# Sparse attention and a rational-activation MLP on one core: the order of the strided casts, and the first and the last group of the MLP in pieces

## The chip, the cores and the metric

The kernel runs on one core of a Trainium2 chip. The metric is the device time of one execution in microseconds (us). A core has five engines that run side by side, each with its own in-order stream of instructions: TensorE (PE, with its weight loads shown apart as PEld), VectorE (DVE), ScalarE (ACT), GpSimd (POOL) and SyncE (SP). Transfers are issued by GpSimd and by SyncE, each with a queue of its own, and are carried out by 16 DMA engines that both queues share.

## The reference

q, k and v have 8 batches, 8 heads, 576 positions and 64 columns. Heads 0 to 3 see a local window, heads 4 to 7 a strided pattern. The result, 4608 tokens of 512 columns, goes through an MLP with 2048 hidden columns and a rational activation.

```python
mask_local = (rel >= 0) & (rel < 32)
mask_strided = (rel >= 0) & (pos[None, :] % 32 == pos[:, None] % 32)
scores = np.where(masks[None, :, :, :], scores, -1000000000.0)
attn = softmax(scores); x = attn @ v          # then heads side by side: 4608 x 512
h = x @ w_in
P = a[0] + a[1] * h + a[2] * h2 + a[3] * h3
Q = 1.0 + np.abs(b[0]) * np.abs(h) + np.abs(b[1]) * h2
g = P / (Q + 1e-06)
return g @ w_out
```

## The kernel before

The kernel is written as a list of operations, each with an engine, an assumed duration, a sort key and the tiles that it reads and writes. `schedule` is a planner: it plays the list on a model of the engines and the DMA queues, always takes the ready operation with the smallest key, and so fixes the order of each engine's stream. `emit` then writes those streams with the semaphore waits that the tiles ask for. The order is therefore fixed before the run; an engine whose next operation isn't ready waits, even if a later one is. A change of one assumed time or one dependence can move operations anywhere in the streams. Where the planner sees TensorE without work at the start or at the end, it puts in filler matmuls on a constant tile (`filler`, L136).

Per batch the work is this:

- `casts(b)` issues on GpSimd the transfers that bring q, k and v in as bf16. For the first two batches q and k of the local heads, then of the strided heads, go straight into SBUF tiles h (L562); for later batches they are copied as bf16 into DRAM (L515). V of the local heads is five transfers (L546 and four times L550), V of the strided heads two (L569). In the kernel before, the five for local V stand between the local pair and the strided pair of q and k.
- `loads(b)` brings q and k into the layout that the scores need (tq, tk). For the first two batches `loads_pe` does it with TensorE transposes (L612, L649), copied out of PSUM by ScalarE for q (L631, L661) and by VectorE for k (L633, L663). For later batches SyncE issues DMA transposes of q and k (L678) and, for the local heads, two small copies each (L689).
- `attention(b)` has four units: local, strided, strided, local. Each computes scores on TensorE (L775 and L784, or L860 and L868), a row maximum on VectorE (L794, L875), subtracts it by a matmul (L801, L882), takes the exponential on ScalarE (L807, L888), transposes it (on TensorE for two batches: L819, L900; then by DMA on SyncE: L825, L908), multiplies with V (L837, L931 with the sums L918), and divides on VectorE (L846 and L848, L938 and L941).
- `turn` transposes the result (L731 local, L738 strided); ScalarE copies it into XT (L754), the tokens side by side in a ring of three chunks of 512.

The MLP takes the tokens in nine chunks of 512 and the hidden columns in four groups of eight blocks. `mlp1(c)` computes a block of h with four matmuls (L966), and ScalarE takes it out of PSUM (L972). When the eight blocks of a group are there, VectorE works on 128 x 4096 elements at once: the absolute value (L992), two operations for the denominator (L994, L996), then ScalarE takes its logarithm and the exponential of the negative (L1020, L1022) while VectorE makes the numerator by Horner's rule (L1023, L1025, L1026, L1027, L1028); L1029 multiplies the two. The last group of the last chunk goes another way: ScalarE takes the absolute value and the first step (L988, L989), the logarithm and exponential are in two halves (L1001, L1003), VectorE does L1004, L1005 and L1006 over the whole, then adds the last coefficient in halves (L1013) and multiplies with the reciprocal in pieces of half, quarter and quarter (L1015). `mlp2(c)` multiplies with w_out (L1055), takes the result out of PSUM (L1067, and L1065 for two pieces of the last chunk) and stores it (L1074). In the last chunk the matmuls are ordered by piece of g, so that they follow the pieces as they become ready.

Of the kernel before, what the change touches and what calls it, by code (L numbers as in the profile page):

```python
# [6 lines left out]
Alu = mybir.AluOpType  # L7
# [362 lines left out]
def bass_strided_sparse_attn__then__act_rational_pade_kernel(nc, q, k, v, moe_w_in, moe_w_out, moe_a, moe_b, out):  # L370
# [163 lines left out]
    def casts(b, after=None):  # L534
        after = after if after else [()] * 7
        key = b * 576 - 1500 if b > 1 else -1e5 + 3e4 * b
        for n in range(2):
            T_q[b][n].new()
            T_k[b][n].new()
        for n in range(2):  # L540
            if n:
                vl = vL_of[b] = R_vL.next()
                vt = vLs_of[b] = vts.setdefault(vl.name, Tile(f"vs{vl.name}")).new()
                va = vl.prev + list(after[2])
                VB = v.offset + b * H * S * D
                P.op("pool", lambda e: e.dma_start(  # L546
                    vl.t[:, 0, :, 0:64], bass.AP(tensor=v.tensor, offset=VB, ap=[[D, KW], [S * D, HL], [1, D]])),
                    0.8, key, w=[vt], dma=0.6, after=va)
                for h in range(HL):
                    P.op("pool", lambda e, h=h: e.dma_start(  # L550
                        vl.t[:, 1:NQ, h, 0:64],
                        bass.AP(tensor=v.tensor, offset=VB + (h * S + STRIDE) * D,
                                ap=[[D, KW], [64 * D, NQ - 1], [1, D]])),
                        0.8, key, w=[vt], dma=0.95, after=va)
            if b < NPE:
                h = stage[b, n] = R_h.next()
                hv = h.t[:, :, :].rearrange("p g c -> p (g c)")
            for i, (s_t, d_t, t) in enumerate(((q, q16, T_q[b][n]), (k, k16, T_k[b][n]))):
                if b >= NPE:
                    bulk(s_t, d_t, b, HL * n, HL, H, t, key, after[3 * n + i])  # L560
                    continue
                P.op("pool", lambda e, s_t=s_t, hv=hv, i=i, n=n: e.dma_start(  # L562
                    hv[0:TP, i * HL * TW:(i + 1) * HL * TW].rearrange("p (h c) -> p h c", c=TW),
                    bass.AP(tensor=s_t.tensor, offset=s_t.offset + (b * H + HL * n) * S * D,
                            ap=[[TW, TP], [S * D, HL], [1, TW]])),
                    0.8, key, w=[t], dma=1.75, after=list(after[3 * n + i]) + h.prev)
        vS = vS_of[b] = R_vS.next()
# [384 lines left out]
    def mlp1(c):  # L952
# [3 lines left out]
        groups = []  # L956
        for g in range(NG):
            h = R_h.next()
            for f in range(g * G, g * G + G):
                ph = PTile("ph", 1)  # L960
                key = base + f * 16
# [8 lines left out]
                if f == 7:  # L970
                    early = o
                P.op("act", lambda e, f=f, ph=ph, h=h: e.activation(  # L972
                    h.t[:, f % G, :], ph.f, AF.Copy),
                     0.6, key, r=[ph], w=[h])
# [7 lines left out]

            def dv(fn, dur, **kw):
                P.op("dve", fn, dur, key, **kw)
            if end:
                y = R_h.next()
                yy = y.t[:, :, :]
                P.op("act", lambda e, zz=zz, hh=hh: e.activation(zz, hh, AF.Abs), 3.6, key, r=[h], w=[z])  # L988
                P.op("act", lambda e, yy=yy, hh=hh: e.activation(yy, hh, AF.Identity, bias=a_ap[2], scale=a_ap[3]),  # L989
                     3.7, key, r=[h, T_co], w=[y])  # L990
            else:
                dv(lambda e, hh=h.t, zz=z.t: e.tensor_scalar(zz.bitcast(u16)[:, :, :], hh.bitcast(u16)[:, :, :], 0x7FFF, None,  # L992
                                                             op0=Alu.bitwise_and), ts + 0.15, r=[h], w=[z])
            dv(lambda e, zz=zz, uu=uu: e.tensor_scalar(uu, zz, b1_ap, b0_ap, op0=Alu.mult, op1=Alu.add),  # L994
               ts + 0.28, r=[z, T_b], w=[u])
            dv(lambda e, zz=zz, uu=uu: e.tensor_tensor(uu, uu, zz, op=Alu.mult), tt, r=[z], m=[u])  # L996
            if end:
                yh = [Tile(f"yh{i}") for i in range(2)]
                for i in range(2):
                    ui = u.t[:, 4 * i:4 * i + 4, :]  # L1000
                    P.op("act", lambda e, ui=ui: e.activation(ui, ui, AF.Ln, bias=eps1, scale=1.0),  # L1001
                         1.9, key, r=[T_co, u], w=[yh[i]])
                    P.op("act", lambda e, ui=ui: e.activation(ui, ui, AF.Exp, scale=-1.0), 1.85, key, m=[yh[i]])  # L1003
                dv(lambda e: e.tensor_tensor(yy, yy, hh, op=Alu.mult), tt, r=[h], m=[y])  # L1004
                dv(lambda e: e.tensor_scalar(yy, yy, a_ap[1], None, op0=Alu.add), ts + 0.22, m=[y])  # L1005
                dv(lambda e: e.tensor_tensor(yy, yy, hh, op=Alu.mult), tt, r=[h], m=[y])  # L1006
                yt = [Tile(f"yt{i}") for i in range(2)]
                for p0, p1 in ((0, 4), (4, 6), (6, 8)):
                    i = p0 // 4
                    tp = Tile(f"hp{p0}")  # L1010
                    if p0 % 4 == 0:
                        yi = y.t[:, p0:p0 + 4, :]
                        dv(lambda e, yi=yi: e.tensor_scalar(yi, yi, a_ap[0], None, op0=Alu.add),  # L1013
                           ts / 2 + 0.22, r=[y], w=[yt[i]])
                    dv(lambda e, p0=p0, p1=p1: e.tensor_tensor(  # L1015
                        h.t[:, p0:p1, :], y.t[:, p0:p1, :], u.t[:, p0:p1, :], op=Alu.mult),
                       tt * (p1 - p0) / G, r=[yt[i], yh[i], h], w=[tp])
                    groups.append((h, p0, p1, tp))
                continue
            P.op("act", lambda e, uu=uu: e.activation(uu, uu, AF.Ln, bias=eps1, scale=1.0),  # L1020
                 0.833 * W / 1000 + 0.28, key, r=[T_co], m=[u])
            P.op("act", lambda e, uu=uu: e.activation(uu, uu, AF.Exp, scale=-1.0), 0.833 * W / 1000 + 0.19, key, m=[u])  # L1022
            dv(lambda e, zz=zz, hh=hh: e.tensor_scalar(zz, hh, a_ap[3], a_ap[2], op0=Alu.mult, op1=Alu.add),  # L1023
               ts + 0.28, r=[h, T_co], m=[z])
# [119 lines left out]
```

## Time and profile before

| | |
|---|---|
| time, median of 3 runs | 405.66 us (403.07 to 407.18) |
| the profiled execution | 407.25 us, span from the first to the last instruction 405.4 us |
| mean granted clock of TensorE | 0.977 |
| VectorE busy | 359.2 us, 89% of the span |
| ScalarE busy | 291.0 us, 72% |
| chain that ended last | VectorE 69%, TensorE 20%, issue 5%, DMA 3% |
| read from and written to HBM | 39.29 MB and 16.52 MB, 138 GB/s over the span |

The profile is of one execution. Busy times are sums over an engine's instructions. The chain that ended last is followed back from the last instruction, at each step to what released it; "issue" in it is time in which an engine waited for nothing that the profile shows. A row of a group gives the line, the engine, the operation and the shapes, the number of instructions, their busy time in us, the mean of one in ns, and the idle time of the engine just before them with what ended most of it. A row of the timeline gives the start and the length in us. A row of a transfer gives its size and the time from issue to landing. Line numbers are those of the kernel before.

### The profile page before, as it was taken

Reading aid. Unit: us, or ns where it says so; the run is one execution under the profiler, and the core shown is the slowest. Engines: PE = TensorE matmul, PEld = TensorE weight load, DVE = VectorE, ACT = ScalarE, POOL = GpSimd, SP = SyncE. Lnnn points to the kernel's source line nnn. Section 1 sums busy time; section 2 is a strip of 40 time slices with the busy share of each in tenths; the row PEclk is TensorE's granted clock in tenths of the full one; section 3 lists DMA queues with packets and bytes.
Section 4 is the critical chain, followed back from the end, with each engine's and each line's share of the span. In section 5 each row is a group of like instructions: output and inputs, shape, how many; then the busy total and the mean of one; then the engine's idle time right before and its main releaser. Section 6 shows DMA issues by size and latency. Waiting matters only on the chain.

```text
span 405.4 us, 8744 instructions
## 1 busy us (share of the span) xinstructions
PE 370.7 (91%) x3874; PEld 184.9 (46%) x3874; DVE 359.2 (89%) x315; ACT 291.0 (72%) x316; POOL 93.6 (23%) x136
## 2 busy tenths in 40 slices
PE   6989774899999999989999999999999999999596
PEld 2463542544554455445444544544454444344242
DVE  4571996799999799999999999999999999999981
ACT  2355593597929695868786878686969888898961
POOL 8991000700171037007213420001000200100100
PEclk9899997899998999999999999999999999999999
DMA  8999999986499939999995997013500200200202
GB/s 100 186 199 176 223 150 98 156 122 129 117 131 165 205 75 146 147 188 150 175 246 82 127 193 173 2 28 110 86 2 27 78 0 28 79 0 27 78 0 103
DMA packets 101638, 45.71 MB, mean 113 GB/s; under 512 B 89184, under 2 KB 97632, under 8 KB 101216
## 3 DMA queue, kind: packets, MB, share of 16 engines
q0 software_dynamic: 41408, 27.93, 45.2%
q1 hardware_dynamic: 60192, 17.22, 28.1%
q8 instruction: 30, 0.49, 0.6%
q14 instruction: 8, 0.07, 0.1%
HBM read 39.29 MB, written 16.52 MB: 138 GB/s over the span
## 4 chain that ended last, share of the span: by engine, by line
DVE 69%; PE 20%; issue 5%; DMA 3%; POOL 2%; ACT 1%; DVEq 0%; POOLq 0%
DVE u L996 9%; DVE z L1025 8%; DVE z L1027 8%; PE PSUM L1055 7%; DVE h L1029 7%; PE PSUM L966 6%; DVE u L994 5%; DVE z L1026 5%; DVE z L1023 5%; DVE z L992 4%; DVE z L1028 4%; DVE xS L941 3%; DVE ng L794 3%; DMA h<-in_k_dram 3%; DVE xL L848 2%
## 5 line engine op out<-in xcount | busy, mean ns | idle before, releaser
L1055 PE MATMUL PSUM<-Wout,h 128*128 128x512 bf16 x576 | 135.1, 382 | 6.3 <-DVE h L1029 4.8
L966 PE MATMUL PSUM<-XT,Win 128*128 128x512 bf16 x576 | 136.8, 385 | 3.9 <-ACT XT L754 1.4
L972 ACT ACTIVATE h<-PSUM 128x512 bf16<-128x512 f32 x144 | 82.4, 600 | 37.6 <-PE PSUM L966 37.4
L1055 PEld LDWEIGHTS PSUM<-Wout,h 128*128 128x128 bf16 x576 | 55.0, 98 | 70.8 <-issue 6.7
L966 PEld LDWEIGHTS PSUM<-XT,Win 128*128 128x128 bf16 x576 | 51.2, 98 | 72.1 <-ACT h L972 13.7
L1020 ACT ACTIVATE u<-u,consts 128x4096 bf16<-128x4096 bf16 x17 | 63.0, 3706 | 12.8 <-DVE u L996 12.8
L1074 POOL DMA_DIRECT2D out_dram<-os x32 | 21.1, 662 | 214.0 <-ACT os L1067 210.8
L1022 ACT ACTIVATE u<-u 128x4096 bf16<-128x4096 bf16 x17 | 61.6, 3623 | 0.2
L996 DVE TENSOR_TENSOR u<-u,z 128x4096 bf16<-128x4096 bf16 x18 | 41.2, 2291 | 0.5
L1027 DVE TENSOR_TENSOR z<-z,h 128x4096 bf16<-128x4096 bf16 x17 | 38.9, 2291 | 0.5
L1025 DVE TENSOR_TENSOR z<-z,h 128x4096 bf16<-128x4096 bf16 x17 | 38.9, 2291 | 0.5
L1029 DVE TENSOR_TENSOR h<-z,u 128x4096 bf16<-128x4096 bf16 x17 | 38.8, 2285 | 0.3
L1067 ACT ACTIVATE os<-PSUM 128x512 f32<-128x512 f32 x34 | 19.7, 603 | 20.0 <-PE PSUM L1055 19.9
L992 DVE TENSOR_SCALAR z<-h 128x4096 uint16<-128x4096 uint16 x17 | 20.8, 1225 | 12.0 <-ACT h L972 11.9
L550 POOL DMA_DIRECT2D vL<-in_v_dram x32 | 29.7, 945 | 0.1
L994 DVE TENSOR_SCALAR u<-z,coef 128x4096 bf16<-128x4096 bf16 x18 | 24.2, 1345 | 0.4
L754 ACT ACTIVATE XT<-PSUM 128x576 bf16<-128x576 bf16 (+2 forms) x40 | 19.8, 558 | 5.2 <-PE PSUM L738 3.6
L1023 DVE TENSOR_SCALAR z<-h,coef 128x4096 bf16<-128x4096 bf16 x17 | 22.7, 1337 | 0.4
L515 POOL DMA_DIRECT2D q<-in_q_dram x12 | 7.3, 608 | 65.7 <-DMA tk<-k 65.3
L1026 DVE TENSOR_SCALAR z<-z,coef 128x4096 bf16<-128x4096 bf16 x17 | 22.1, 1299 | 0.4
L1028 DVE TENSOR_SCALAR z<-z,coef 128x4096 bf16<-128x4096 bf16 x17 | 21.8, 1283 | 0.4
L136 PE MATMUL PSUM<-FL 128*128 128x512 bf16 x74 | 20.3, 428 | 1.5 <-DVE FL L501 1.5
(79 smaller groups left out, 380.3 us busy)
## 6 DMA issues: line engine op xcount, KB each, us to landing
out_dram<-os POOLq DMA_DIRECT2D x32, 256.0 KB, 2.8
q<-in_q_dram POOLq DMA_DIRECT2D x12, 288.0 KB, 5.7
k<-in_k_dram POOLq DMA_DIRECT2D x12, 288.0 KB, 6.9
vL<-in_v_dram POOLq DMA_DIRECT2D x32, 96.0 KB, 5.1
vS<-in_v_dram POOLq DMA_DIRECT2D x16, 144.0 KB, 8.6
Win<-in_moe_w_in_dram POOLq DMA_DIRECT2D x8, 256.0 KB, 12.8
Wout<-in_moe_w_out_dram POOLq DMA_DIRECT2D x4, 512.0 KB, 23.9
h<-in_q_dram POOLq DMA_DIRECT2D x4, 288.0 KB, 13.5
```

The source lines that it names most:

```text
L966: r = e.matmul(ph.f, Win[:, kk, f * 128:(f + 1) * 128], XT[:, kk, xc:xc + CH], start=(kk == 0), stop=(kk == NK1 - 1))
L972: P.op("act", lambda e, f=f, ph=ph, h=h: e.activation(h.t[:, f % G, :], ph.f, AF.Copy), 0.6, key, r=[ph], w=[h])
L994: dv(lambda e, zz=zz, uu=uu: e.tensor_scalar(uu, zz, b1_ap, b0_ap, op0=Alu.mult, op1=Alu.add), ts + 0.28, r=[z, T_b], w=[u])
L996: dv(lambda e, zz=zz, uu=uu: e.tensor_tensor(uu, uu, zz, op=Alu.mult), tt, r=[z], m=[u])
L1020: P.op("act", lambda e, uu=uu: e.activation(uu, uu, AF.Ln, bias=eps1, scale=1.0), 0.833 * W / 1000 + 0.28, key, r=[T_co], m=[u])
L1022: P.op("act", lambda e, uu=uu: e.activation(uu, uu, AF.Exp, scale=-1.0), 0.833 * W / 1000 + 0.19, key, m=[u])
L1023: dv(lambda e, zz=zz, hh=hh: e.tensor_scalar(zz, hh, a_ap[3], a_ap[2], op0=Alu.mult, op1=Alu.add), ts + 0.28, r=[h, T_co], m=[z])
L1025: dv(lambda e, zz=zz, hh=hh: e.tensor_tensor(zz, zz, hh, op=Alu.mult), tt, r=[h], m=[z])
L1026: dv(lambda e, zz=zz: e.tensor_scalar(zz, zz, a_ap[1], None, op0=Alu.add), ts + 0.22, m=[z])
L1027: dv(lambda e, zz=zz, hh=hh: e.tensor_tensor(zz, zz, hh, op=Alu.mult), tt, r=[h], m=[z])
L1029: dv(lambda e, zz=zz, hh=hh, uu=uu: e.tensor_tensor(hh, zz, uu, op=Alu.mult), tt, r=[z, u], m=[h])
L1055: r = e.matmul(po.f, h.t[:, j, m * 128:(m + 1) * 128], Wout[:, kk, :], start=(kk == 0), stop=(kk == NF - 1))
```

## The change

It has three parts. In `casts` the five transfers of local V move behind the loop that issues q and k, so that the strided pair of q and k comes directly behind the local pair; this holds for all batches.

```diff
         for n in range(2):
-            if n:
-                vl = vL_of[b] = R_vL.next()
-                vt = vLs_of[b] = vts.setdefault(vl.name, Tile(f"vs{vl.name}")).new()
-                va = vl.prev + list(after[2])
...
             if b < NPE:
                 h = stage[b, n] = R_h.next()
...
+        vl = vL_of[b] = R_vL.next()
+        vt = vLs_of[b] = vts.setdefault(vl.name, Tile(f"vs{vl.name}")).new()
+        va = vl.prev + list(after[2])
+        VB = v.offset + b * H * S * D
+        P.op("pool", lambda e: e.dma_start(
...
         vS = vS_of[b] = R_vS.next()
```

In `mlp1` the first group of the first chunk (`cut`) does its absolute value and the two operations of the denominator in halves of four blocks, the first half as soon as its four blocks are out of PSUM. The logarithm, the exponential and the numerator stay whole.

```diff
+            cut = c == 0 and g == 0
+            hf = [Tile(f"hf{i}") for i in range(2)]
...
-                     0.6, key, r=[ph], w=[h])
+                     0.6, key, r=[ph], w=[h, hf[f % G // 4]])
...
+            if cut:
+                zu = [Tile(f"zu{i}") for i in range(2)]
+                for i in range(2):
+                    hi, zi, ui = (x.t[:, 4 * i:4 * i + 4, :] for x in (h, z, u))
+                    dv(lambda e, hi=hi, zi=zi: e.tensor_scalar(zi.bitcast(u16), hi.bitcast(u16), 0x7FFF, None,
+                                                               op0=Alu.bitwise_and), ts / 2 + 0.15, r=[hf[i]], w=[zu[i]])
+                    dv(lambda e, ui=ui, zi=zi: e.tensor_scalar(ui, zi, b1_ap, b0_ap, op0=Alu.mult, op1=Alu.add),
+                       ts / 2 + 0.28, r=[T_b], m=[zu[i]])
+                    dv(lambda e, ui=ui, zi=zi: e.tensor_tensor(ui, ui, zi, op=Alu.mult), tt / 2 + 0.08, m=[zu[i]],
+                       r=[])
```

In the last group of the last chunk (`end`), the third multiplication (L1006), the last addition (L1013) and the product (L1015) are done piece by piece, in four pieces of two blocks, instead of whole, in two halves, and in a half and two quarters.

```diff
-                dv(lambda e: e.tensor_tensor(yy, yy, hh, op=Alu.mult), tt, r=[h], m=[y])
-                yt = [Tile(f"yt{i}") for i in range(2)]
-                for p0, p1 in ((0, 4), (4, 6), (6, 8)):
-                    i = p0 // 4
+                    yt = [Tile(f"yt{i}") for i in range(4)]
+                    for p0, p1 in ((0, 2), (2, 4), (4, 6), (6, 8)):
+                        i = p0 // 2
                         tp = Tile(f"hp{p0}")
+                        yi, hi = y.t[:, p0:p1, :], h.t[:, p0:p1, :]
+                        dv(lambda e, yi=yi, hi=hi: e.tensor_tensor(yi, yi, hi, op=Alu.mult), tt / 4 + 0.12, r=[h, y],
+                           w=[yt[i]])
                         dv(lambda e, yi=yi: e.tensor_scalar(yi, yi, a_ap[0], None, op0=Alu.add),
-                           ts / 2 + 0.22, r=[y], w=[yt[i]])
+                           ts / 4 + 0.22, m=[yt[i]])
                         dv(lambda e, p0=p0, p1=p1: e.tensor_tensor(
                             h.t[:, p0:p1, :], y.t[:, p0:p1, :], u.t[:, p0:p1, :], op=Alu.mult),
-                       tt * (p1 - p0) / G, r=[yt[i], yh[i], h], w=[tp])
+                           tt * (p1 - p0) / G + 0.12, r=[yt[i], yh[i // 2], h], w=[tp])
```

Since the planner works on the whole list, the order of all streams changes with these edits, also where the list itself is the same. In the changed kernel TensorE's stream has the first strided scores of batch 2 (L868) ahead of the strided transposes of batch 1 (L738), where it has them behind in the kernel before; the fillers between the last two runs of output matmuls are one instead of nine.

More of the change, by code (lines that the diff above doesn't have):

```diff
@@ L540, in casts @@
         for n in range(2):
-            if n:
-                vl = vL_of[b] = R_vL.next()
-                vt = vLs_of[b] = vts.setdefault(vl.name, Tile(f"vs{vl.name}")).new()
-                va = vl.prev + list(after[2])
[L545 to L554, printed above, removed]
             if b < NPE:
@@ L566, in casts @@
                     0.8, key, w=[t], dma=1.75, after=list(after[3 * n + i]) + h.prev)
+        vl = vL_of[b] = R_vL.next()
[3 more added lines that the diff above has]
+        P.op("pool", lambda e: e.dma_start(
+            vl.t[:, 0, :, 0:64], bass.AP(tensor=v.tensor, offset=VB, ap=[[D, KW], [S * D, HL], [1, D]])),
+            0.8, key, w=[vt], dma=0.6, after=va)
+        for h in range(HL):
+            P.op("pool", lambda e, h=h: e.dma_start(
+                vl.t[:, 1:NQ, h, 0:64],
+                bass.AP(tensor=v.tensor, offset=VB + (h * S + STRIDE) * D,
+                        ap=[[D, KW], [64 * D, NQ - 1], [1, D]])),
+                0.8, key, w=[vt], dma=0.95, after=va)
         vS = vS_of[b] = R_vS.next()
```

69 lines of the change are left out of this document (37 added, 32 removed).

## The prediction

> **What bounds the kernel now.** I read the busy shares first, then the chain of waits, then the busy time by stage, and last the rows of the two stages that the change touches. The page gives VectorE 89% of the span. PE's 91% holds filler matmuls (L136) and waiting time, so its share says less.
>
> ```profile
> PE 370.7 (91%) x3874; PEld 184.9 (46%) x3874; DVE 359.2 (89%) x315; ACT 291.0 (72%) x316; POOL 93.6 (23%) x136
> ```
>
> By stage (stretch; length, then PE, PEld, DVE, ACT and POOL busy, granted clock, DMA share, GB/s):
>
> ```profile
> 41.32:60.90 19.58, 15.22 (x306) 9.01 (x306) 19.39 (x24) 15.05 (x20) 0.00 (x0) 1.00 1.42 185
> 60.90:77.00 16.10, 9.11 (x142) 5.77 (x142) 9.75 (x12) 7.41 (x11) 3.96 (x6) 0.79 1.09 117
> 77.00:384.10 307.10, 294.51 (x2842) 143.71 (x2842) 299.92 (x231) 241.84 (x251) 59.11 (x82) 0.99 0.63 105
> ```
>
> From 77 us to 384.1 us VectorE works 299.92 of 307.10 us: it is the bound, and what happens before is worth exactly what it lets VectorE do sooner. Two places remain where it idles: the time before 41.32 us, and 16.10 − 9.75 = 6.35 us in the stretch 60.9 to 77. After 384 us the end is set by PE. The chain of waits (start, length, what) names the pieces:
>
> ```profile
> 7.43 11.11 DMA h<-in_k_dram
> ...
> 33.57 7.09 PE PSUM L966 x32
> ...
> 61.48 5.89 issue
> ...
> 384.09 8.53 PE PSUM L1055 x32
> 392.61 1.94 PE PSUM L136 x9
> 394.55 6.92 PE PSUM L1055 x32
> ```
>
> The reader is to see three things: the strided k of batch 0 is waited for until 18.54 us; PE stands 5.89 us at 61.48 us on nothing that the profile shows; and at the end nine fillers stand on the chain between the last two runs of output matmuls.
>
> **Part 1, strided q and k ahead of local V, batch 0.** In the GpSimd queue five V transfers stand ahead of the strided pair:
>
> ```profile
> 2.94 0.70 POOL L546 DMA_DIRECT2D vL<-in_v_dram  x1
> ...
> 3.62 3.10 POOL L550 DMA_DIRECT2D vL<-in_v_dram  x4
> ...
> 7.43 0.73 POOL L562 DMA_DIRECT2D h<-in_k_dram  x1
> ...
> 15.83 2.22 DVE L794 TENSOR_REDUCE ng<-PSUM 128x10 bf16<-128x960 f32 x2 [2.15 <-PE PSUM L784]
> ...
> 22.08 0.51 PE L837 MATMUL PSUM<-vL,ptL 96*64 96x65 bf16 x20
> ```
>
> The pair is issued 0.70 + 3.10 = 3.8 us sooner, so k lands near 18.54 − 3.8 = 14.7 us (estimate). Not all of that reaches the end of attention 0. Today the two local maxima (L794, 2.22 us of VectorE) run while k is awaited; in the planned order of the changed kernel they stand behind the copy of strided k. So 3.8 − 2.2 = 1.6 us are left: the first MLP matmul goes from 33.57 to about 32.0 us. Bounds: 0 (the new order of attention 0 loses what it wins) and 3.8. I take 1.6, since the displaced work is that row. V is issued two cast issues later (2 × 0.73 us) and has 4.1 us more of transfer ahead of it at most, by this row for its last piece (issued 5.95, landed 14.4):
>
> ```profile
> vL<-in_v_dram POOLq DMA_DIRECT2D x1, 96.0 KB, 8.4
> ```
>
> 14.4 + 4.1 = 18.5 us is still 3.6 us ahead of its reader L837 at 22.08, which the change hardly moves. So this costs nothing; beyond those 3.6 us each us later is one us of attention 0. For batch 1 the same swap lies beside MLP matmuls that last until 40.6 us; nothing.
>
> **Part 2, the first group in halves.** VectorE today waits for all eight evictions L972:
>
> ```profile
> 34.65 0.60 ACT L972 ACTIVATE h<-PSUM 128x512 bf16<-128x512 f32 x1 [1.13 <-PE PSUM L966]
> ...
> 40.69 0.60 ACT L972 ACTIVATE h<-PSUM 128x512 bf16<-128x512 f32 x1 [0.27 <-PE PSUM L966]
> 41.32 1.23 DVE L992 TENSOR_SCALAR z<-h 128x4096 uint16<-128x4096 uint16 x1 [9.62 <-ACT h L972]
> ```
>
> (40.69 − 34.65) / 7 = 0.86 us each, so the first half is ready 4 × 0.86 = 3.45 us sooner. Prices of whole, half and quarter operations stand in the groups kept apart by shape (busy, mean ns):
>
> ```profile
> L996 DVE TENSOR_TENSOR u<-u,z 128x4096 bf16<-128x4096 bf16 x18 | 41.2, 2291 | 0.5
> L994 DVE TENSOR_SCALAR u<-z,coef 128x4096 bf16<-128x4096 bf16 x18 | 24.2, 1345 | 0.4
> L992 DVE TENSOR_SCALAR z<-h 128x4096 uint16<-128x4096 uint16 x17 | 20.8, 1225 | 12.0 <-ACT h L972 11.9
> L1013 DVE TENSOR_SCALAR h<-h,coef 128x2048 bf16<-128x2048 bf16 x2 | 1.5, 750 | 0.0
> L1015 DVE TENSOR_TENSOR h<-h,u 128x1024 bf16<-128x1024 bf16 x2 | 1.3, 689 | 0.0
> L1005 DVE TENSOR_SCALAR h<-h,coef 128x4096 bf16<-128x4096 bf16 x1 | 1.3, 1286 | 0.0
> L1015 DVE TENSOR_TENSOR h<-h,u 128x2048 bf16<-128x2048 bf16 x1 | 1.2, 1227 | 0.0
> ```
>
> A half costs about 0.72 + 0.78 + 1.23 = 2.73 us (the scalar ones scaled by 750/1286). The first half is over 0.7 us before the second half of h is there. From the last eviction on, today's work is 1.23 + 1.35 + 2.29 = 4.87 us, then 2.73: 2.1 us won, with the three extra instructions (0.6 us) inside that sum. Bounds 1.5 and 2.7. With part 1 VectorE leads by 1.6 + 2.1 = 3.7 us. ScalarE's Ln and Exp (L1020, L1022) now both stand ahead of the softmax of batch 1, where today only Ln does. If that makes batch 1's attention late, it costs only what exceeds the gate of part 3, ahead of which it stands.
>
> **Part 3, what is late next: the stretch 60.9 to 77.** With no wait the second group's first operation would go from 77.03 to 77.03 − 3.7 − 6.35 = 67.0 us. The planned order shows what can hold it. For batches from 2 on, the strided k cast is now issued ahead of V, and the planner, which believes it lands sooner, puts batch 2's first strided scores (L868) ahead of the strided transposes (L738) of batch 1 and of twelve MLP matmuls, and their maximum (L875) right behind the second group's first operation. Both engines work in order, so both wait there for strided tk of batch 2.
>
> ```profile
> 25.47 0.65 POOL L515 DMA_DIRECT2D q<-in_q_dram  x1
> ...
> 30.07 0.53 POOL L515 DMA_DIRECT2D k<-in_k_dram  x1
> ```
>
> ```profile
> k<-in_k_dram POOLq DMA_DIRECT2D x1, 288.0 KB, 36.0
> ```
>
> ```profile
> 59.77 7.24 SPq L678 DMA_TRANSPOSE tq<-q  x1
> ...
> 68.33 1.83 SPq L678 DMA_TRANSPOSE tk<-k  x1
> ```
>
> ```profile
> tk<-k SPq DMA_TRANSPOSE x1, 4.3
> ```
>
> The cast of k landed at 30.07 + 36.0 = 66.1 us and will land several us sooner. But its transpose stands on SyncE behind the one of q, whose issue ends at 67.0 us, and then takes 4.3 us. The two local copies (L689, 1.23 us) no longer stand between: about 70.5 to 71.3 us instead of 72.6. I take 70.5. Scores (1.0) and maximum (0.75) end near 72.2; the two operations that today precede that maximum (L994, L996) follow, 3.7 us: 75.9.
>
> ```profile
> 81.89 0.75 DVE L875 TENSOR_REDUCE ng<-PSUM 100x16 bf16<-100x576 f32 x1
> ```
>
> Today the same work is done at 82.64: a lead of 6.7 us. Bounds: 10.1 us if the transpose lands before it is wanted (67.0 + 1.2 + 0.75 + 3.6 = 72.5), 4.6 us if it lands at 72.6 as now. The PE wait of 5.89 us may come again at 60 us; it ended at 67.4 and what stands behind it (3 us) fits ahead of the same gate, so it costs little more.
>
> A row decides between the two bounds: the transpose of q took 7.24 us to issue while casts were in flight, that of k 1.83 us after. The Trainium skill ("DMA: Bandwidth & Descriptors", section "Queues, rings and completion order") says that each DMA engine takes turns between the queues that have work, a packet at a time; by it an order changed inside GpSimd's queue does not take its share away from the transposes' time, and the lead would be nearer the smaller bound, as I have it.
>
> **Part 4, 77 to 384 us.** VectorE's operations are the same, 7.18 us idle. The planner deals all of them out anew, so small waits come and go: 0, between −3 and +3 us, less than half of that idle time either way. Casts of batches 3 to 7 have strided q and k sooner and V later by 4 to 5 us of issue; GpSimd's queue is otherwise waiting for outputs.
>
> **Part 5, the last group in four pieces.** Its DVE chain from L1006 becomes four times (quarter multiply, quarter add, quarter multiply).
>
> ```profile
> 387.87 2.29 DVE L1006 TENSOR_TENSOR h<-h 128x4096 bf16<-128x4096 bf16 x1
> ...
> 389.95 1.91 ACT L1003 ACTIVATE u<-u 128x2048 bf16<-128x2048 bf16 x1
> ```
>
> A quarter add is about 0.750 − 0.536/2 = 0.48 us (estimate), a piece 0.69 + 0.48 + 0.69 = 1.86. Ready at 389.7, 391.6, 393.4, 395.3 us; the second Exp ends at 391.86 in time for the third. PE finishes the group before at 392.6, runs one filler instead of nine (1.94 → 0.22) and then 8 matmuls per piece, 6.92 / 4 = 1.73 us each: the last piece starts at 398.0, well after 395.3. VectorE ends 1.1 us later than today, behind PE. Saved: 1.94 − 0.22 = 1.7 us; bounds 0 and 1.9.
>
> **Sum.** −6.7 − 1.7 + 0 = −8.4 us. The profiled execution took 407.25 us (span 405.4); the median of the runs is 405.66, 0.4% less. That gives 398.85 against its own time and 397.3 against the median. I take the middle, 406.45 − 8.4 = 398.0, and the same base for the rivals.
>
> **Rivals.** (a) Half the lead is lost: PE's wait comes again and delays batch 1, or the new order meets 3 us more waits after 77. Lead 4.6 − 3 + 1.7 = 3.3: 403.1. For it: the chain has four such issue waits of over 1 us after 77, the first and the last of them
>
> ```profile
> 142.01 1.35 issue
> ...
> 297.86 1.45 issue
> ```
>
> and each could come back longer. Against it: VectorE is rarely without work there. (b) Slower: strided k of batch 2 gates PE and VectorE much later. If the cast keeps its 36.0 us (26.0 + 36.0 = 62.0), then the 7.24 us issue, then the slowest landing of such a transpose,
>
> ```profile
> tq<-q SPq DMA_TRANSPOSE x1, 14.1
> ```
>
> 62.0 + 7.2 + 14.1 = 83.3 us. Each us after 70.5 costs one: 12.8 − 8.4 = 4.4 us slower, 410.8. It decides from a landing at 79 us. Against it: the sooner cast, and the 4.3 us above. (c) No hole at all: PE's wait does not return and the transposes are early: 10.1 + 1.7 = 11.8, so 394.6. This is where a rule comes in. Row first:
>
> ```profile
> q8 instruction: 30, 0.49, 0.6%
> ```
>
> 0.49 MB in 30 packets is 16 KB each, and the 5.89 us wait stands inside a run of equal matmuls without a semaphore; I read it as PE out of instructions while DMA was full. The Trainium skill ("Runtime: NRT & Kernel Launch", section "Instruction fetch mechanics") says that instructions come in 16 KiB blocks and that crossing one is mostly hidden. The packet size agrees, the wait does not; by the rule, case (c).
>
> **Numbers.** Forecast 0.56, (a) 0.19, (b) 0.12, (c) 0.13. About 1% (4.06 us) is what a measurement of this kernel tells from none: below 401.6 is faster, above 409.7 slower. Faster: 0.56 + 0.13 and a little of (a): 0.70. Slower: 0.12. Same: 0.18. The range 392.0 to 405.0 holds the forecast, (c) and nearly all of (a).
>
> **What would show it.** Right: k of batch 0 lands near 14.7 us; the first L966 at 32 us; VectorE's first half at 36.5 us; less than 4 us idle between 60 and 75 us, ended by strided tk of batch 2; one filler and gapless output matmuls at the end, 1.7 us shorter. Wrong: a landing of that tk after 75 us, a PE issue wait of over 3 us behind 62 us, or more than 10 us of VectorE idle time after 77 us.

## The result, and the profile after

The changed kernel took 402.35 us (median of 20 runs, 400.02 to 406.88), the kernel before beside it 407.53 us (20 runs, 403.07 to 411.03): ratio 0.9891, 95% interval 0.9863 to 0.992. The forecast of 398.0 us was 4.35 us too low; its range held the time, and rival (a), 403.1 us, came nearest. The profiled execution of the changed kernel took 405.59 us (span 403.8), that of before 407.25 us (span 405.4). A ratio counts only the executions of each kernel within 1.5% of its shortest, and since times of the kernel before are spread widely (on one chip below, 6 of 17 from 399.4 to 403.0 us and 11 from 405.5 to 410.1), ratios and medians can differ, and both are given.

One correction to the description above: a chunk has 2048 / 128 = 16 hidden blocks, so two groups of eight and not four, 18 groups in all.

The sharpest view is the busy time by stage (stretch; length, then PE, PEld, DVE, ACT and POOL busy, granted clock, DMA share, GB/s). The kernel before:

```profile
0.00:77.00 77.00, 58.78 (x961) 33.90 (x962) 48.05 (x75) 40.22 (x60) 34.53 (x55) 0.93 1.34 161
77.00:140.00 63.00, 61.00 (x645) 30.48 (x645) 59.73 (x48) 46.43 (x52) 15.23 (x21) 0.97 0.93 145
140.00:200.00 60.00, 57.46 (x763) 30.57 (x762) 59.21 (x53) 45.70 (x49) 19.98 (x28) 1.00 1.11 143
200.00:260.00 60.00, 58.91 (x612) 28.53 (x611) 59.20 (x50) 45.44 (x51) 13.68 (x17) 1.00 0.83 150
260.00:320.00 60.00, 58.36 (x556) 28.88 (x553) 58.83 (x48) 48.26 (x53) 5.45 (x8) 1.00 0.21 52
320.00:384.10 64.10, 58.79 (x271) 25.25 (x271) 62.96 (x36) 56.01 (x48) 4.78 (x8) 1.00 0.10 38
```

The changed kernel:

```profile
0.00:77.00 77.00, 63.38 (x1025) 38.35 (x1026) 54.76 (x83) 41.32 (x61) 37.11 (x58) 0.89 1.36 168
77.00:140.00 63.00, 60.90 (x694) 30.47 (x692) 60.36 (x52) 48.61 (x56) 16.73 (x24) 0.97 1.15 167
140.00:200.00 60.00, 57.80 (x656) 29.87 (x655) 59.02 (x49) 45.02 (x46) 16.12 (x22) 0.97 0.87 139
200.00:260.00 60.00, 58.08 (x706) 30.32 (x704) 55.85 (x50) 45.26 (x52) 12.70 (x17) 1.00 0.70 123
260.00:320.00 60.00, 57.94 (x455) 27.82 (x454) 55.59 (x43) 45.80 (x49) 6.03 (x8) 0.97 0.18 52
320.00:384.10 64.10, 58.95 (x272) 25.33 (x271) 62.83 (x37) 56.37 (x49) 4.76 (x8) 1.00 0.10 37
```

Read the DVE column downwards and keep a running difference. VectorE does the same work in both kernels (0.6 us more after, for the extra instructions of the halves), so a difference is a lead. At 77 us the changed kernel leads by 54.76 − 48.05 = 6.7 us, at 200 us by 6.7 + 0.63 − 0.19 = 7.2 us. Then it loses 3.35 us from 200 to 260 and 3.24 us from 260 to 320 us, and at 384 us the lead is 348.41 − 347.98 = 0.4 us. VectorE stands idle for 13.45 us from 77 to 384 us, against 7.18 us before. The change won what was forecast and gave nearly all of it back 130 to 240 us later, in code that it doesn't touch. From 200 to 260 us the granted clock is 1.00 in both kernels, so what is lost there isn't lost to half clock.

Where it was given back stands in the timeline of VectorE, after (start, length, line; in brackets the idle time before it and what ended it):

```profile
257.81 1.16 DVE L793 TENSOR_REDUCE ng<-PSUM 128x10 bf16<-128x960 f32 x1 [1.77 <-PE PSUM L783]
...
289.73 2.29 DVE L1045 TENSOR_TENSOR z<-z,h 128x4096 bf16<-128x4096 bf16 x1
291.94 0.25 DVE L937 RECIPROCAL rc<-PSUM 100x16 f32<-100x16 f32 x1
...
300.64 1.23 DVE L1010 TENSOR_SCALAR z<-h 128x4096 uint16<-128x4096 uint16 x1 [3.61 <-ACT h L973]
```

and of TensorE, after:

```profile
292.25 3.19 PE L1073 MATMUL PSUM<-Wout,h 128*128 128x512 bf16 x8 [1.69 <-DVE rc L937]
```

The other waits of VectorE from 200 to 320 us are 0.8 us or shorter. In the kernel before its longest wait from 140 to 320 us is

```profile
281.42 1.16 DVE L794 TENSOR_REDUCE ng<-PSUM 128x10 bf16<-128x960 f32 x1 [0.29 <-PE PSUM L784]
```

The reader is to see a loop through two engines: the reciprocal L937 stands behind a 2.29 us product, TensorE's output matmuls wait 1.69 us for it (the planner gave them the PSUM bank that it reads), the next hidden blocks come later for that, and VectorE waits 3.61 us for them at 300.64.

The places that the prediction named. The first MLP matmul, and the gate in the stretch 60.9 to 77 us, on TensorE after:

```profile
33.85 2.33 PE L967 MATMUL PSUM<-XT,Win 128*128 128x512 bf16 x10 [0.36 <-ACT XT L753]
...
70.13 0.42 PE L859 MATMUL PSUM<-MS,IDN 128*128 128x288 bf16 x2 [2.09 <-DMA tk<-k]
```

The first half of the first group on VectorE after (41.32 us before):

```profile
38.14 0.69 DVE L990 TENSOR_SCALAR z<-h 128x2048 uint16<-128x2048 uint16 x1 [6.09 <-ACT h L973]
```

And the end of the chain of waits after, with one filler between the two runs, too short for a line of its own:

```profile
383.94 8.75 PE PSUM L1073 x32
392.91 6.92 PE PSUM L1073 x32
```

### The profile page after: what moved, and what is told of

Same layout as the page of the kernel before. It is cut to its first block, busy times and chain, and to the rows that moved or that the text cites. A ratio compares the mean times of both kernels' runs of the same rounds, so it can differ in the third digit from the quotient of the medians.

```text
span 403.8 us, 8723 instructions
## 1 busy us (share of the span) xinstructions
PE 372.8 (92%) x3859; PEld 188.7 (47%) x3859; DVE 360.6 (89%) x324; ACT 291.1 (72%) x316; POOL 93.5 (23%) x136
## 4 chain that ended last, share of the span: by engine, by line
DVE 53%; PE 20%; DMA 9%; ACT 7%; POOL 6%; issue 3%; SPq 3%; POOLq 0%
PE PSUM L1073 9%; DVE u L1014 8%; DMA q<-in_q_dram 7%; PE PSUM L967 7%; DVE z L1043 6%; DVE h L1047 5%; DVE z L1045 5%; DVE u L1012 5%; DVE z L1010 4%; DVE z L1041 4%; DVE z L1044 3%; DVE z L1046 3%; SPq L677 2%; ACT u L1040 2%; DVE xS L940 2%
## 5 line engine op out<-in xcount | busy, mean ns | idle before, releaser
L967 PEld LDWEIGHTS PSUM<-XT,Win 128*128 128x128 bf16 x576 | 52.5, 99 | 71.7 <-ACT h L973 12.6
L1038 ACT ACTIVATE u<-u,consts 128x4096 bf16<-128x4096 bf16 x16 | 59.3, 3706 | 8.1 <-DVE u L1014 7.8
L1040 ACT ACTIVATE u<-u 128x4096 bf16<-128x4096 bf16 x16 | 57.9, 3621 | 0.1
L1045 DVE TENSOR_TENSOR z<-z,h 128x4096 bf16<-128x4096 bf16 x17 | 38.9, 2290 | 0.5
L1014 DVE TENSOR_TENSOR u<-u,z 128x4096 bf16<-128x4096 bf16 x17 | 38.9, 2289 | 0.4
L1085 ACT ACTIVATE os<-PSUM 128x512 f32<-128x512 f32 x34 | 19.9, 603 | 24.8 <-PE PSUM L1073 24.7
L561 POOL DMA_DIRECT2D vL<-in_v_dram x32 | 26.6, 855 | 0.0
L806 ACT ACTIVATE pL<-PSUM 128x960 bf16<-128x960 f32 x16 | 15.4, 968 | 13.1 <-PE PSUM L800 13.1
L1010 DVE TENSOR_SCALAR z<-h 128x4096 uint16<-128x4096 uint16 x16 | 19.5, 1221 | 5.4 <-ACT h L973 5.4
L1012 DVE TENSOR_SCALAR u<-z,coef 128x4096 bf16<-128x4096 bf16 x17 | 22.8, 1342 | 0.3
L793 DVE TENSOR_REDUCE ng<-PSUM 128x10 bf16<-128x960 f32 x16 | 18.3, 1151 | 4.2 <-PE PSUM L783 4.2
L1041 DVE TENSOR_SCALAR z<-h,coef 128x4096 bf16<-128x4096 bf16 x16 | 21.5, 1344 | 0.5
```

The lines of the kernel that those rows point to most:

```text
L967: r = e.matmul(ph.f, Win[:, kk, f * 128:(f + 1) * 128], XT[:, kk, xc:xc + CH], start=(kk == 0), stop=(kk == NK1 - 1))
```

## The experiments

Three theories went into the runs. A: TensorE is the second bound and can't follow a VectorE that leads. B: the lead goes into stretches of half TensorE clock. C: the order that the planner deals anew for all streams wins or loses by itself. "Before" is the kernel before, run on the same chip beside the kernel in question; differences of two kernels are those of their means with two standard errors. More than one chip was used, so a time is best compared with the times beside it.

**The parts.** The tail alone: the casts in their old place, and `cut = False`, so that the first group is whole.

```diff
-            cut = c == 0 and g == 0
+            cut = False
```

> Only the last group in four pieces; casts and first group as before, and every stream has the order of the kernel before up to its last operations. The step of the prediction on the tail (1.7 us, 1.6 us seen in the pair of profiles): 1.7 us shorter, ratio 0.996, TensorE from the product of the group before to its last matmul 15.7 us instead of 17.4. Rival, the gain of the tail is an accident of one profile: ratio 1.000.

The casts alone: the kernel before with the moved loads of the diff and nothing else.

> Only strided q and k ahead of local V; first and last group whole as before. Theory A (VectorE's lead is real but TensorE, the second bound, can't follow it after 200 us): VectorE leads the kernel before by 2 to 5 us of work at 77 us and by under 1.5 us at 320 us; ratio 0.996 to 1.000. Theory B (the lead is lost to extra spells of half TensorE clock): the loss after 77 us is 1.7 us for each such spell that the kernel before hasn't; without extra spells the lead stays and the ratio is 0.990. Theory C (the order dealt anew wins or loses by itself): anything from 0.985 to 1.01, not tied to the lead at 77 us.

The halves alone (the casts and the tail as before), and casts with halves (only the tail as before):

> Only the first MLP group's first operations in halves; casts and the last group as before. The step of the prediction: 2.1 us of lead at 45 us. Theory A: the lead is gone by 320 us, ratio 0.998 to 1.000. Theory B: the lead stays but for 1.7 us for each added spell of half clock. Theory C: not tied to the lead.

> The change without its third part (the last group whole). All theories: slower than the whole change by the 1.7 us of the tail. So against the kernel before, with the whole change at 0.989: 0.993. Under theory A VectorE's lead in work is 6 to 7 us at 77 us and 200 us and under 1.5 us at 320 us, as in the profile of the whole change; under theory B executions with fewer spells of half clock are faster by 1.7 us for each.

| kernel | median us (runs) | ratio to before, 95% |
|---|---|---|
| before | 406.33 (35) | |
| tail | 401.77 (12) | 0.995, 0.9908 to 0.9991 |
| casts | 398.99 (12) | 0.9907, 0.9864 to 0.9949 |
| halves | 404.64 (12) | 0.9986, 0.9937 to 1.0034 |
| casts and halves | 403.31 (12) | 0.9997, 0.996 to 1.0033 |

The tail's expected ratio, 0.996, lies in its interval. The halves alone win nothing clear of noise, and casts with halves miss the 0.993 that all theories expected. Halves put on top of the casts cost 4.3 ± 1.2 us, while their first operation starts at 38 us as in the whole change. Theory A falls here: the casts alone hold their lead. Their stages:

```profile
200.00:260.00 60.00, 58.01 (x701) 30.30 (x702) 58.95 (x52) 46.32 (x53) 12.10 (x16) 1.00 0.71 119
260.00:320.00 60.00, 58.08 (x456) 27.17 (x455) 59.23 (x45) 50.57 (x48) 4.41 (x8) 1.00 0.17 51
```

TensorE's share is that of the whole change (58.0 us in each), and VectorE has 3.1 and 3.6 us more done. Casts and halves wait where the whole change waits (1.77 us for L783 at 254.4, 3.62 us for h at 297.2).

**Parts without the halves, and halves without a new order.** Casts and tail (`cut = False` alone). Then the same with the first three VectorE operations of the first group cut by hand after the order is dealt, so that every other operation keeps its place:

```diff
     P.schedule()
+    dv3 = [x[0] for x in P.first[:3]]
...
+    od = [o for o in od if o not in new]
+    od[at:at] = [new[o][i] for i in range(2) for o in dv3]
+    P.order["dve"] = od
```

> The casts moved and the tail in four pieces, without the halves. Casts alone were 398.99 us against 406.3 (ratio 0.9907), the tail alone took 1.6 us in the profiles. All theories expect the sum, 396.5 to 398, a ratio near 0.985: nothing in either part touches the other in time. If it comes out above 399, the two share something that has not been seen.

> Casts and tail as in the run beside it, with the order that the planner dealt for that one kept on every engine; only VectorE's first three MLP operations are cut into halves, by hand, after the order is dealt. Theory C (the order dealt anew loses the lead, not the halves): the halves keep part of their 2.1 us, 395 to 397.5, not slower than the run beside it by more than 0.5. Theory A (TensorE can't follow a lead that is larger than the casts' 6 us): equal to the run beside it within 0.7. A fourth theory, that halves cost by themselves (three more VectorE operations, copies of tk behind them): slower than the run beside it by 1 us or more.

Measured: 397.54 us (12 runs) and 397.53 us (6 runs), before 406.96 us (29 runs); ratios 0.9856 (0.9802 to 0.9911) and 0.9878 (0.9812 to 0.9944). Casts and tail lie within their expectation. The halves show neither a cost nor a gain: 0.0 ± 1.6 us. Their 2 us end at the gate of Part 3, as a row of TensorE with the halves cut by hand suggests, a wait for strided tk of batch 2:

```profile
69.62 0.42 PE L859 MATMUL PSUM<-MS,IDN 128*128 128x288 bf16 x2 [3.02 <-DMA tk<-k]
```

So the 4.3 us above are not a price of the halves; they are a price of the order dealt with them.

**One place of the order mended.** The whole change, and after the planner is done the three operations behind L1045 at 289.7 us go ahead of it (`P.cube` lists the L1045 of all groups):

```diff
     P.schedule()
+    od = P.order["dve"]
+    k = od.index(P.cube[11])
...
+    od[k:k + 4] = od[k + 1:k + 4] + [od[k]]
```

> The whole change with one place of VectorE's order mended by hand: the strided reciprocal and its two products that stood behind the 2.29 us product at 289.7 us go ahead of it; every other engine's order stays. Theory C: TensorE's 1.69 us wait before its output matmuls at 292 us goes, with it most likely the half clock stretch from 292.9 us (1.3 us of matmul time), and VectorE's 3.61 us wait at 300.6 us shrinks to 1 or less; VectorE pays 0.5 to 0.8 us for waiting for the strided sums at 289.7. Sum 1.5 to 3 us: 399.3 to 401 against 402.35 for the whole change. Theory A: TensorE has the work to do in any order, the wait comes back elsewhere before 320 us, 402.3 within 0.8. Theory B: only what the half clock stretch took comes back, 0.5 to 1.3 us.

Measured: 400.53 us (12 runs), ratio 0.9943 (0.9894 to 0.9991), within theory C's range; the whole change beside it comes with the next runs. VectorE with the place mended:

```profile
289.89 0.26 DVE L937 RECIPROCAL rc<-PSUM 100x16 f32<-100x16 f32 x1 [0.53 <-PE PSUM L917]
290.36 1.29 DVE L940 TENSOR_TENSOR xS<-PSUM,rc 100x512 bf16<-100x512 f32 x2 [0.21 <-PE PSUM L930]
...
297.88 1.23 DVE L1010 TENSOR_SCALAR z<-h 128x4096 uint16<-128x4096 uint16 x1 [0.38 <-ACT h L973]
```

It pays 0.53 + 0.21 us as expected, the 3.61 us wait is down to 0.38, the next group starts 2.8 us sooner, and from 260 to 320 us VectorE gets 58.06 us done instead of 55.59. The half clock stretch there is gone too, so for this place C and B are one chain: the order opens TensorE's gap, the gap brings the clock down.

**A second place.** The same, and two copies of h ahead of the Exp that starts at 246 us; beside it the whole change once more:

```diff
+    od = P.order["act"]
+    k = [i for i, o in enumerate(od) if round(o.dur, 3) == round(0.833 * 4.096 + 0.19, 3)][9]
...
+    od[k:k + 3] = od[k + 1:k + 3] + [od[k]]
```

> The whole change with the place at 290 us mended as before and a second one: on ScalarE two copies of hidden blocks go ahead of the Exp that starts at 246 us, so that TensorE need not wait 1.24 us for them at 250 us. Theory C: VectorE's waits at 257.8 (1.77) and 259.4 us (0.42) shrink together by 1 to 1.5 us, VectorE's lead at 320 us rises from 3.4 to 4.5 us or more over the kernel before, and the time is 1 us below the one with one place mended: 399 to 400. If the wait at 257.8 has another source (the order of TensorE's own matmuls there), nothing moves: 400.5.

> The whole change as it is, on the same chip as the other three, as their companion: 402.35 within 0.7. Its profile should have VectorE's waits at 257 and 300 us again (theory C), whatever its clock does elsewhere; if they are absent in this execution, they were an accident of one profile and theory C falls.

Measured on one chip: 400.42 us (12 runs) with two places mended, 402.71 us (12 runs) for the whole change, a difference of 2.5 ± 1.1 us. The second mend is a miss: VectorE's wait stands as it was:

```profile
255.29 1.16 DVE L793 TENSOR_REDUCE ng<-PSUM 128x10 bf16<-128x960 f32 x1 [1.77 <-PE PSUM L783]
```

and the time is that of one place mended. TensorE's wait for the copies at 250 us is gone, but it now waits 0.94 us for VectorE's L847 at about the same place. So the copies aren't the source of VectorE's wait; that TensorE's own order is, as the expectation has it, is not shown. The whole change has its waits again in this second profile, 1.77 us at 257.3 and 3.62 us at 300.1 us: they belong to the order, not to one execution. Its ratio to before on this chip is 1.0017 (0.9976 to 1.0058): no gain; a possible reason comes below.

**Other orders, no instruction altered.** The planner is told that one Ln takes 0.20 us longer, or that every copy of a hidden block takes 0.62 in place of 0.60 us; the second also in the kernel before.

```diff
-                     0.833 * W / 1000 + 0.28, key, r=[T_co] + zu, w=[u])
+                     0.833 * W / 1000 + 0.48, key, r=[T_co] + zu, w=[u])
```

```diff
-                     0.6, key, r=[ph], w=[h, hf[f % G // 4]])
+                     0.62, key, r=[ph], w=[h, hf[f % G // 4]])
```

> The whole change with one number of the planner altered and no instruction: the logarithm of the first group is assumed to take 0.20 us longer. The order is dealt otherwise on all engines from there on. Theory C: the time moves by more than 1 us against 402.35, to either side, anywhere from 396 to 407. Theories A and B (the work or the clock sets it, not the order): 402.35 within 1 us.

> The whole change with the same number altered (0.62 for 0.60), no instruction. Theory C: again a time of its own; if VectorE's lead at 200 us (7.2 us) lasts to 320 us as in the other order that was dealt for it (399.2), 397 to 400; if places like those at 257 and 292 us come again, 401 to 404. Theory A: 402.35 within 1.

> The kernel before with one number of the planner altered and no instruction: the copy of a hidden block out of PSUM is assumed to take 0.62 us in place of 0.60. Theory C: VectorE has no lead to lose in before (it waits 0.29 us in 140 to 320 us), so a new order can only lose there: 405.5 to 410; it could gain only in the first 77 us. If the order alone makes gains as large as this change's, it would come below 403.

| kernel | median us (runs) | before beside it | ratio, 95% |
|---|---|---|---|
| whole change, Ln 0.20 longer | 399.17 (12) | 406.96 (29) | 0.991, 0.9866 to 0.9954 |
| whole change, copies 0.62 | 396.62 (6) | 406.07 (17) | 0.9893, 0.9852 to 0.9935 |
| before, copies 0.62 | 399.48 (13) | 406.07 (17) | 0.9935, 0.9894 to 0.9976 |

The same instructions, dealt three ways, take 402.35 (measured again 402.71), 399.17 and 396.62 us. They were not measured side by side; on one chip, the change as it is and its 0.62 order with the fillers described below are 5.6 ± 1.3 us apart. Theories A and B, which expected 402.35 within 1 us, don't explain this by themselves. The 0.62 order keeps what it has won:

```profile
200.00:260.00 60.00, 58.52 (x672) 30.18 (x671) 58.28 (x50) 45.62 (x55) 14.25 (x16) 1.00 0.66 109
260.00:320.00 60.00, 59.67 (x468) 28.98 (x467) 59.01 (x44) 49.93 (x49) 6.09 (x8) 1.00 0.23 56
```

My expectation for the kernel before was wrong: by the ratio it too gains by another order (runs of 397.3 to 399.5 and of 405.7 to 410.2 us), though the means of all runs, 403.0 and 405.1 us, are not told apart by the noise.

**Casts by hand.** The kernel before, its order kept on all engines, only GpSimd's loads swapped after the order is dealt:

```diff
+    ops = list(P.ops)
     P.schedule()
+    od = P.order["pool"]
+    for i in P.late:
+        vload, strided = ops[i:i + 5], ops[i + 5:i + 7]
...
+        od[at:at] = strided + vload
```

> The kernel before with nothing altered but the order of GpSimd's loads: in every batch the strided q and k load goes ahead of the five local V loads, by hand, after the order of all engines has been dealt, so every engine keeps the order of before. If the casts' gain of 7 us lies in the data that come sooner (my Part 1 and Part 3): 399 to 402.5. If it lies in the order that the planner deals with them (theory C carried over to the casts): 405 to 408, equal to before within 1 us, or slower where local V comes too late for an order that was dealt for it.

Measured: 405.15 us (6 runs, 404.15 to 411.97), ratio 1.0121 (1.004 to 1.0202). By the medians it is 0.9 us shorter than before (406.07 us), by the ratio longer; either way the 7 us of the casts aren't there. The six runs speak for theory C: data that come sooner were worth little in an order that wasn't dealt for them. TensorE in this kernel:

```profile
32.56 7.08 PE L966 MATMUL PSUM<-XT,Win 128*128 128x512 bf16 x32 [0.28 <-ACT XT L754]
...
64.45 0.24 PE L918 MATMUL PSUM<-ONE,ptS 128*128 128x2 bf16 x4 [3.93 <-issue]
```

The first MLP matmul comes 1.0 us sooner than before (33.57), near Part 1's 1.6.

**Fillers.** 12 more fillers in the first 11 us, in three kernels: casts and tail, the kernel before, and the whole change with the 0.62 order.

```diff
-                    n = int((t - free[e]) * 0.7 / 0.216) if free[e] > 0 else 16
+                    n = int((t - free[e]) * 0.7 / 0.216) if free[e] > 0 else 20
...
+    P.filler(8, free[-1], None, 0.0)
+    od.insert(at, od.pop())
```

> Casts and tail, in the order dealt for them (397.5 us), with filler matmuls, whose results nobody reads, in TensorE's two waits before the first k arrives: 20 in place of 16 at the start, and 8 more behind the first q transposes. If the half clock stretch from 12.3 to 19.1 us there comes from those waits (1.4 and 2.1 us), it goes, the first MLP matmul comes at 31.5 to 32.5 in place of 33.4 us, and the time is 396 to 397. If the fillers delay the k transposes, or something other than TensorE's clock holds the first 33 us (VectorE, ScalarE, the transposes by DMA), 397.5 or up to 1 us more.

> The kernel before, its order kept, with 12 more filler matmuls in the first 11 us (20 in place of 16 at the start, 8 more behind the first q transposes). If TensorE's wait near 62 us depends on where in TensorE's instruction stream its next piece of code ends while the casts fill the DMA queues, 12 matmuls (0.1 of a piece of 128) move it, and it goes or shrinks below 1 us: 399 to 402, and the profile has no issue wait above 1.5 us between 55 and 75 us. If it hangs on the work that stands there, or on the casts alone, it stays at 3 to 6 us after matmul 856 and the time stays at 405 to 408.

> The whole change in its second other order (0.62 us assumed for the copies, 396.6 us), with the 12 more fillers. In that order VectorE keeps its lead and the profile has no wait of TensorE above 2.3 us, so there is little left to win: 395.5 to 397. If the half clock stretch at 11.9 us (6.8 us long) goes without another in its place, up to 1.6 us less, 395; if the fillers move a fetch into the path, 398 to 400.

| kernel with fillers | median us (runs) | without them | ratio to before, 95% |
|---|---|---|---|
| casts and tail | 396.26 (6) | 397.54, another chip | 0.9896, 0.9839 to 0.9954 |
| before | 402.12 (12) | 401.51 (29) | 1.0001, 0.9959 to 1.0042 |
| whole change, 0.62 | 397.06 (6) | 396.62, another chip | 0.9891, 0.9824 to 0.9957 |

For casts and tail the time fell within its expectation, but not for its reason: the half clock stretch at 12.3 us is gone, TensorE stands elsewhere instead, and the first MLP matmul is later (33.36 us without the fillers).

```profile
20.07 0.34 PE L867 MATMUL PSUM<-tk,tq 64*36 64x36 bf16 x14 [2.77 <-issue]
...
34.26 2.12 PE L967 MATMUL PSUM<-XT,Win 128*128 128x512 bf16 x9 [0.36 <-ACT XT L753]
```

What it gained in the profile it gained at 65 us, where casts and tail have this row, and the fillers leave no wait above 1.5 us there:

```profile
64.81 0.61 PE L930 MATMUL PSUM<-vS,ptS 36*36 36x64 bf16 x29 [3.29 <-issue]
```

In the kernel before, the fillers' profile has no such wait either, but on that chip the kernel before without them rarely has long times (21 of 29 runs below 403.2 us, 5 above 405), and 3 of 12 runs with fillers are above 405 as well. Whether fillers drive the wait out stays open.

The lowest median is that of casts and tail with fillers, 396.26 us, with the whole change in the 0.62 order, 396.62 us, measured beside it: 0.1 ± 1.5 us apart, both below the change as it is and the kernel before.

## Why the prediction missed

**What bounds: right, with a weak base.** VectorE is the bound, and its busy time by stage shows where the change wins and loses. But 5.89 us of the base were an issue wait of one execution. The kernel with the tail alone has 3.71 us there, the kernel before with 0.62 has 5.45, and both come after the same number of matmuls as in before, 856:

```profile
66.08 0.24 PE L918 MATMUL PSUM<-ONE,ptS 128*128 128x2 bf16 x4 [3.71 <-issue]
```

```profile
69.50 1.87 PE L966 MATMUL PSUM<-XT,Win 128*128 128x512 bf16 x4 [5.45 <-issue]
```

The profile of before with fillers, which has no such wait, spans 400.4 us, 5.0 less than that of before. That the short and the long executions of before are those without and with this wait fits, but is only argued: no short execution of before itself was profiled. It would explain the two verdicts on the whole change: 0.9891 where before took 407.53 us, 1.0017 where it took 401.51.

**Part 1, mis-sized: −1.6 us, measured +0.3 us.** Strided k landed about as forecast (its transposes start at 14.86 us, forecast 14.7), but the transposes of local q and k came later, at 8.45 and 11.82 us (7.99 and 10.10 before), and the clock fell. From 13.1 to 19.9 us, before and after:

```profile
13.10:19.90 6.80, 6.05 (x118) 3.06 (x117) 3.38 (x5) 2.35 (x6) 6.80 (x11) 0.86 1.27 191
```

```profile
13.10:19.90 6.80, 6.80 (x113) 3.82 (x113) 5.27 (x10) 1.32 (x4) 6.80 (x11) 0.52 1.93 179
```

The first MLP matmul came at 33.85 instead of 32.0 us. By hand, in before's order, the same swap gave 1.0 us. That the clock is what took it in the new order isn't shown, since the fillers put another wait in its place.

**Part 2: right at its place.** 38.14 instead of 41.32 us (forecast 36.5, with a gain of Part 1 that didn't come), halves at 0.69, 0.81 and 1.22 us (2.72; forecast 2.73). But the run with the halves cut by hand shows no gain at the end (0.0 ± 1.6 us), and its wait at Part 3's gate is the likely reason.

**Part 3: right.** The gate is strided tk of batch 2 at 70.13 us (forecast 70.5), VectorE's lead at 77 us 6.7 us (forecast 6.7). VectorE came to the gate later than forecast (the second group's first operation at 69.14 us, forecast 67.0) and waited 1.47 us there, so the gate also hid Part 1's miss. The rule of the Trainium skill on turns between queues ("DMA: Bandwidth & Descriptors", section "Queues, rings and completion order") spoke for a lead nearer the smaller bound of 4.6 to 10.1 us; the 6.7 us agree with it, but no run tells it from the order on SyncE alone.

**Part 4, the step that failed: "0, between −3 and +3".** 6.3 us of lead went between 77 and 384 us in the profiled execution, and VectorE's idle time there, 13.45 us, is above the 10 us that the prediction itself gave as a sign of being wrong. Mending the place at 290 us (with the second mend, which moved nothing) was worth 2.5 ± 1.1 us of time. The step priced the new order by the idle time of the old one (7.18 us), as if the old order were a sample of what the planner deals. It is not: three orders of one and the same list of instructions differ by up to 5.7 us. The profiled execution of the changed kernel is also one of its longest (405.59 against a median of 402.35), so that the typical loss is less than 6.3 us: the forecast's 8.4 us less the 5.2 us between the medians leaves 3.2 us. The rest of that execution's length may go with its clock: over the 20 executions the time rises as the granted clock falls (correlation −0.73), and the profiled one has 0.960 where their mean is 0.968. Whether half clock itself lengthens an execution (theory B) or comes from the same waits stays open.

**Part 5: right.** From the start of the last two runs of output matmuls to their end it was 8.53 + 1.94 + 6.92 = 17.4 us before and is 15.9 us after, 1.5 us shorter (forecast 1.7).

**Rivals.** (a) was the outcome, by its second condition ("the new order meets 3 us more waits after 77"); with the waits known to come by order, it deserved more than 0.19. (c) had half of its condition: the changed kernel has no issue wait above 1.5 us between 55 and 77 us, but tk wasn't early and gated the stretch. (b) fell with tk of batch 2 at 70.13 us, well before its 79. The rule of the Trainium skill ("Runtime: NRT & Kernel Launch", section "Instruction fetch mechanics") that was cited for (c) is not confirmed by the missing wait: kernels with other orders still have it.

## What to carry to other kernels

Where a planner deals an order, an edit is two changes: its own, and a new deal. Price the second by dealing the unedited list a few times with an assumed duration moved by a few per cent, before believing a gain or a loss of 1%; here that alone moved the time of the changed kernel by up to 5.7 us. A lead of the bound engine is worth what is left of it at the end: follow the running difference of its busy time stage by stage, and look for the small operation that stands behind a long one while another engine waits for its buffer.

## What the runs showed of the hardware

- A long wait without a releaser came after the same number of matmuls, 856 as counted in the trace, in the kernel before, with the tail alone, with the casts alone, with the casts by hand and in the kernel before with the 0.62 order, at three different operations, with 5.89, 3.71, 2.18, 3.93 and 5.45 us; with casts and tail it came after 850, with 3.29 us. In all six a packet of the instruction queue (q8) ends inside the wait, 1.4 to 2.2 us before TensorE goes on. In the kernel before this packet starts at 61.84 us and takes 3.36 us; the changed kernel has one from 61.23 us that takes 1.36 us, and no such wait. So I read the wait as TensorE out of instructions; it was not tested by itself. The Trainium skill ("Runtime: NRT & Kernel Launch", section "Instruction fetch mechanics") lets instruction blocks be crossed mostly hidden; by this reading one crossing in the stretch full of casts was not, and its price differed by 3.7 us between kernels that run the same work.
- In the trace of the changed kernel TensorE's clock is halved five times before 300 us. Four of these stretches, of 6.8, 3.4, 10.2 and 3.4 us, start 0.4 to 1.7 us after the ends of waits of 2.14, 1.98, 2.09 and 1.69 us; the fifth starts at 183.5 us behind no wait above 0.5 us in the 9 us before. Not every such wait brings one: in the changed kernel's second profile a wait of 2.21 us at 83.5 us is followed by none. The stretch behind the 1.69 us is the one where the place at 290 us opens its gap; 8 output matmuls take 3.19 us there, and 7 take 1.67 us in the kernel with that place mended:

```profile
292.90:296.30 3.40, 3.40 (x21) 1.80 (x20) 3.37 (x4) 0.78 (x3) 0.00 (x0) 0.53 0.02 5
```

The Trainium skill ("TensorE: Matmul & The Clock Gate", section "What's actually happening") has the clock fall after at least one idle window of about 3.4 us. The length of the stretch agrees with such a window, while a wait of half a window was enough here.
